# A fused attention, RWKV mix and FFT feed-forward kernel on one core: two variance products placed later, the rows of one pair reordered, and joint visits from group 7 on

## The chip, the core and the metric

The program runs on one core of one Trainium2 chip. The metric is the device time of one launch in microseconds (us). Runs of one program agree within some tenths of a per cent.

## What is computed

The sizes are B = 4 batches, 12 heads, S = 448 tokens, D = 768, and hidden widths of 1024 and 3072. All is float32.

```python
attn = 1 / (1 + exp(-(scale * q @ k.T - log(S))));  x = attn @ v          # per head, heads side by side
xk = mu_k * x + (1 - mu_k) * x_prev;  xr = mu_r * x + (1 - mu_r) * x_prev  # x_prev: one token earlier
x = sigmoid(xr @ w_r) * (relu(xk @ w_k) ** 2 @ w_v)
u = x + real(fft(fft(x, axis=1), axis=2))
un = (u - mean(u)) / sqrt(var(u) + 1e-6)
out = u + relu(un @ w_ch1) @ w_ch2
```

## The kernel before

Tokens lie in the free dimension (448 columns), features in the partitions, in blocks of 128. Nearly every product is done on operands split in two float32r parts, high and low, as three matmuls (high by high, high by low, low by high). A split is one cast on ScalarE (ACT) and one subtraction on VectorE (DVE).

**The order of the work** is written by a planner, the class `Order` (line 136). Pieces of the program are generators. `Order.run` (line 184) wakes those whose time has come on a clock of its own, `now`, and between them issues one matmul of the queue `feed`. A generator yields the time at which it wants to be woken. Each engine executes what was issued to it in exactly that order, whatever the real times are; the real waits are semaphores that come from the data. `need` (line 162) yields until the planner's time of a step, `issued` (line 169) only until the step has been issued. So a number that is yielded moves instructions in the queues of PE, ACT, DVE and SP (which issues the transfers), and nothing else.

**The stages**, in order of time: attention with the key products `k`, the receptance products `r`, the value products `v`, the Fourier part, the normalisation, the first feed-forward product `f`, and the second one `m`. The value products of batches 0 to 3 run from 343 us on, with the Fourier work of the batch before among them.

*The value and Fourier part, per batch b.* `val_done` (line 832) multiplies a finished `v` tile by the receptance tile `rv`, loaded by `load_r` (line 784), which frees the tile's PSUM bank. `folds` (line 880) forms the operands `xf`, `yf` on DVE and their parts `xh`, `xl`, `yh`, `yl`. `spectrum` (line 970) issues the matmuls `pa`, `qa` (on those parts), `pq`, `sp`, then the product `mu` with a matrix of ones, for the mean. `centre` (line 1039) subtracts the mean, squares, and adds the squares up in `sum_v`. `scale` (line 1073) splits `sum_v` into a tile `sq`, issues the two matmuls `var` with the ones, and computes `rs` = 1/sqrt by one ACT function and one Newton step on DVE. Then `centre` multiplies six blocks by `rs` (`x<-x,rs`), one after the other, each waiting for the one before. For batch 1, `load_un` (line 774) splits each of these blocks into `un`, the operand of the next stage. The ones at lines 1079 and 1080 are what the change touches.

*The first feed-forward product.* There are 12 groups of 256 hidden columns (`NG`). Groups 0 to 3 (`PL = 4`) of batches 0 and 1 are done plainly (`plain`, line 1342, tiles named `f`, 18 matmuls each): 16 tiles. All else runs on pairs of batches with Strassen's scheme, seven products of half-size blocks instead of eight: pair 0 is batches 0 and 1, pair 1 is batches 2 and 3. A visit is one group for one pair (63 matmuls) or for both (126 matmuls, a joint visit). The list `VISITS` (line 131) holds visits of pair 0 alone (groups `PL` to `JO`-1), then joint visits (groups `JO` to 11), then visits of pair 1 alone (groups 0 to `JO`-1); before, `JO` is 8. `visit_loads` (line 1276) fetches a group's weights, 2 tiles `a` of 384 KB. `visits` (line 1296) forms sums of their blocks on DVE (`s`, `a`) and splits the seven operands `blk`. It is a generator of its own, so it prepares the first two operands of visit 0 as soon as their weights have landed. `plain_done` and `after` (line 1367) move results from PSUM through ACT and DVE to staging tiles `h`, `w`, `u`, and store them (`h_d`). The staging tiles of pair 1 have one buffer each.

*The rows of a pair* are the other operands. `rows0` (line 1200) prepares pair 0. `rows1` (line 1232) prepares pair 1 from whole half-batches of 1344 columns: B11 and B21 as they are, then T1, T3, T2 and T4 from differences, and B22. Its helper `split` waits for the cast, then for the subtraction, before the next step is issued. T4 and B22 go through DRAM (`t_d`), since their place is needed.

*The second part of the weights.* `convert_rest` (line 1644) rewrites 48 halves of w_ch2 (raw 384 KB each) into operands `v_d` in DRAM. It starts when visit `JO - PL` has its second weight tile, with at least 3.5 us from one half to the next on the planner's clock. When the last product of pair 0 is done (`LAST0`, line 132, the end of visit 7), the loads for the second product (`w`, `r`) and three more places for weights of visits are set free at once.

Of the kernel before, what the change touches and what calls it, by code (L numbers as in the profile page):

```python
# [12 lines left out]
F32 = mybir.dt.float32  # L13
F32R = mybir.dt.float32r
# [3 lines left out]
ALU = mybir.AluOpType  # L18
# [3 lines left out]
B, H, S, DH = 4, 12, 448, 64  # L22
# [4 lines left out]
KD = D // 128  # L27
# [10 lines left out]
NV = 3  # L38
TURNS = (2, 4)
EVERY = (9.0, 10.3)  # L40
PL, JO, EARLY = 4, 8, 8

SL = np.r_[np.arange(2, 129, 2), np.arange(1, 128, 2)]
LL = np.r_[0, np.arange(130, 255, 2), np.arange(129, 256, 2)]
# [236 lines left out]
def build(tc, ap):  # L281
    nc = tc.nc
    V, G = nc.vector, nc.gpsimd
    o = Order(nc)
    est = ExitStack()

    def pool(stack, name, bufs=1, side="left", space=None):
        if space is not None:
            return stack.enter_context(tc.tile_pool(name=name, bufs=bufs, space=space))
        return stack.enter_context(tc.tile_pool(name=name, bufs=bufs, side=side, reuse_waits="tile"))  # L290

    def shift(pl, name, n=1):
        pl.tile([128, int(16 * n)], F32, tag=f"shift_{name}", name=f"shift_{name}", bufs=1)
# [70 lines left out]
    t_d = [dram.tile([128, 3, S], F32, name=f"t_d{i}") for i in range(2)]  # L364
# [259 lines left out]
    for f in range(NF + KD):  # L624
        if f < NF:
            src, hl, key = ap["w_k"][f], [w[:, f].rearrange(flat) for w in (wkh, wkl)], ("wk", f)
        elif f < NF + HELD:
            src, hl, key = ap["w_r"][f - NF], [w.rearrange(flat) for w in wr_t[f - NF]], ("wr", f - NF)
# [46 lines left out]
    def bank2(name):  # L675
        return ps1b.tile([128, 512], F32, tag="bank2", name=name)
# [73 lines left out]
    def split(t, key, raw):  # L750
        yield o.act(t[:, 0], raw)
        o.at[key] = o.sub(V, t[:, 1], raw, t[:, 0])
        yield o.now
# [53 lines left out]
    np_ = pool(s_r, "norm", 1, "right")  # L807
# [67 lines left out]
    def ft(b, tag, shape, dtype=F32, bufs=1, pl=None):  # L875
        return (pl or fp).tile(shape, dtype, tag=tag, name=f"{tag}_{b}", bufs=bufs)
# [162 lines left out]
    def centre(b, ps):  # L1039
# [6 lines left out]
        for i in range(3):  # L1046
# [12 lines left out]
            yield o.act(sq, xx, AF.Square)  # L1059
            add_up(b, "v", i, sq)  # L1060
        yield from scale(b)
        rs = rs_t[b]
        for i in range(KD):
# [9 lines left out]
    def scale(b):  # L1073

        yield from o.need(("v", b, 2))
        hl = ft(b, "sq", [128, 2, S], F32R, pl=np_)
        v = sp_t[b]["v"]
        yield o.act(hl[:, 0], v)
        yield o.sub(V, hl[:, 1], v, hl[:, 0])
        ps = bank2(f"var_{b}")  # L1080
        for c in range(2):
            o.mm(ps[:, 0:S], one, hl[:, c], c == 0, c == 1)
        yield o.now + 0.1
        vs = ft(b, "sq", [128, 2, S], pl=np_)
        vv, sd = vs[:, 0], vs[:, 1]
        rs = rs_t[b] = np_.tile([128, S], F32, tag="rsb", name=f"rs_{b}", bufs=1)
        yield o.ts(vv, ps[:, 0:S], 1.0 / D, 1e-6, ALU.mult, ALU.add)
        o.spend(nc.scalar, 1.3)
        yield o.act(rs, vv, AF.Abs_reciprocal_sqrt)
        yield o.act(sd, rs, AF.Square)  # L1090
        o.tt(V, sd, sd, vv, ALU.mult)
        o.ts(sd, sd, -0.5, 1.5, ALU.mult, ALU.add)
        t = o.tt(V, rs, rs, sd, ALU.mult)
        o.at["scaled", b] = o.now
        yield t
# [5 lines left out]
    blk_t, t_t, plain_t = {}, {}, {}  # L1101
# [48 lines left out]
    def quarter(name, dtype=F32R):  # L1150
        return wq.tile([128, D], dtype, tag="wq", name=name, bufs=4)
# [79 lines left out]

    def rows1():
        def split(nm, hi, lo, src):
            yield o.act(hi, src)
            t = o.sub(V, lo, src, hi)
            for d in range(3):
                t_t[1, nm, d] = (hi[:, d], lo[:, d])
                o.at["t", 1, nm, d] = t
            yield t

        def new(nm):
            t = tp1.tile([128, 2, 3, S], F32R, name=f"{nm}_1")
            return t[:, 0], t[:, 1]

        yield from o.need(("centre", 2))
        u = x2_t[2]
        b11, b21 = u[:, 0:3], u[:, 3:6]
        yield from split("B11", *new("B11"), b11)
        yield from split("B21", *new("B21"), b21)
        yield from o.need(("centre", 3), ("rows", 0))  # L1250
        v = x2_t[3]
        b12, b22 = v[:, 0:3], v[:, 3:6]
        o.dma(t_d[1], b22)
        yield o.tt(V, b11, b12, b11, ALU.subtract)
        t1 = np_.tile([128, 2, 3, S], F32R, tag="x2", name="T1_1", bufs=3)
        yield from split("T1", t1[:, 0], t1[:, 1], b11)
        yield o.tt(V, b12, b22, b12, ALU.subtract)
        yield from split("T3", *new("T3"), b12)
        yield o.tt(V, b12, b22, b11, ALU.subtract)
        yield from split("T2", *new("T2"), b12)  # L1260
        yield o.tt(V, b21, b21, b12, ALU.subtract)
        yield o.dma(t_d[0], b21) + 2.0
        for i, nm in enumerate(("T4", "B22")):
            t = np_.tile([128, 2, 3, S], F32R, tag="x2", name=f"{nm}_1", bufs=3)
            yield o.dma(t[:, 1].bitcast(F32), t_d[i]) + 0.5
            yield from split(nm, t[:, 0], t[:, 1], t[:, 1].bitcast(F32))
        shift(tp1, "tp1")
        o.at["rows", 1] = o.now

    wt_t, place_t = {}, {}  # L1270
    for v, (g, ps) in enumerate(VISITS):
        for j in range(2):
            i = 2 * (v - NG + PL) + j
# [22 lines left out]
    def visits():  # L1296

        n = D // 2
        for v in range(len(VISITS)):
            yield from o.need(("wt", v, 0), ("wt", v, 1))  # L1300
            wa, wb = wt_t[v, 0], wt_t[v, 1]
            a11, a12, a21, a22 = wa[:, 0:n], wa[:, n:D], wb[:, 0:n], wb[:, n:D]
            s3 = al.tile([128, n], F32, tag="sw", name=f"s34_{v}", bufs=1)
            src = {"A11": a11, "S2": a11, "S3": s3, "S1": a21, "A12": a12, "A22": a22, "S4": s3}
            t = {"S3": o.tt(V, s3, a11, a21, ALU.subtract), "S1": o.tt(V, a21, a21, a22, ALU.add)}
            for k, (nm, _, _) in enumerate(PRODUCTS):
                m = 7 * v + k
                yield t.get(nm, o.now)
                if m > 5:
                    yield from o.need(("prod", m - 6))  # L1310
                elif m > 1:
                    yield from o.need("plain loads", ("pl", 2 * PL - 2 + (m > 3), 1, KD - 1))
                if m % 6 < 2:
                    blk = alb.tile([128, D], F32R, tag="blk", name=f"blk_{m}", bufs=2)
                else:
                    blk = quarter(f"blk_{m}")
                blk_t[m] = blk
                yield o.act(blk[:, 0:n], src[nm])
                o.at["blk", m] = o.sub(V, blk[:, n:D], src[nm], blk[:, 0:n])
                if nm == "A11":  # L1320
                    t["S2"] = o.tt(V, a11, a21, a11, ALU.subtract)
                elif nm == "A12":
                    o.at["wt free", v, 0] = t["S4"] = o.tt(V, s3, a12, a11, ALU.subtract)
                elif nm == "A22":
                    o.at["wt free", v, 1] = o.at["blk", m]
        o.at["visits"] = o.now
# [274 lines left out]
    o.spawn(rows0())  # L1601
    o.spawn(visit_loads())
    o.spawn(visits())
    o.spawn(network())
    o.run(("four", B - 1))
    s_f.close()
    s_b = ExitStack()
    tp1 = pool(s_b, "tp1", 1, "right")
# [44 lines left out]

    o.spawn(convert_rest())
    o.spawn(rows1())
    o.run(("prod", LAST0))
    s_t.close()
# [85 lines left out]
```

## Time and profile before

| | us |
|---|---|
| median of three runs (1141.53 to 1143.3) | 1141.82 |
| the profiled execution | 1139.96 |
| its span, first to last instruction | 1138.2 |
| PE busy in the span | 1118.6 (98%) |
| PE weight loads busy | 975.0 (86%) |
| DVE busy | 810.6 (71%) |
| ACT busy | 649.2 (57%) |

Some 1.8 us of the profiled execution lie around its span. The 5908 matmuls are pipelined, each has a busy time longer than its distance to the next, so a stall is read from the starts of neighbouring matmuls, or from the column of the idle time, and not from the busy share. The granted clock is at its upper level (2.4 GHz, written 1.00) but for two stretches, read below at 0.50 (1.2 GHz).

### The profile page before, as it was taken

Reading aid. Unit: us, or ns where it says so; the run is one execution under the profiler, and the core shown is the slowest. Engines: PE = TensorE matmul, PEld = TensorE weight load, DVE = VectorE, ACT = ScalarE, POOL = GpSimd, SP = SyncE. Lnnn points to the kernel's source line nnn. Section 1 sums busy time; section 2 is a strip of 40 time slices with the busy share of each in tenths; the row PEclk is TensorE's granted clock in tenths of the full one; section 3 lists DMA queues with packets and bytes.
Section 4 is the critical chain, followed back from the end, with each engine's and each line's share of the span. In section 5 each row is a group of like instructions: output and inputs, shape, how many; then the busy total and the mean of one; then the engine's idle time right before and its main releaser. Section 6 shows DMA issues by size and latency. Waiting matters only on the chain.

```text
span 1138.2 us, 16784 instructions
## 1 busy us (share of the span) xinstructions
PE 1118.6 (98%) x5908; PEld 975.0 (86%) x5908; DVE 810.6 (71%) x1306; ACT 649.2 (57%) x1165; POOL 16.1 (1%) x49
## 2 busy tenths in 40 slices
PE   9999999999999999989999999989999999999998
PEld 3476676799999989979999999879999999999997
DVE  3876767566624678799896565677657679976887
ACT  6788877766632333334686666667755444554442
POOL 0000001100000000000000000000000000000000
PEclk9999999999999999999999999999999999999999
DMA  7765789667939786536967988999887448945432
GB/s 247 237 231 202 241 325 342 256 231 262 335 136 313 278 305 226 179 134 227 298 230 249 301 300 276 319 318 360 271 332 267 135 151 283 360 145 184 160 99 86
DMA packets 116309, 279.65 MB, mean 246 GB/s; under 512 B 13248, under 2 KB 58496, under 8 KB 116096
## 3 DMA queue, kind: packets, MB, share of 16 engines
q1 hardware_dynamic: 113472, 266.29, 68.4%
q0 software_dynamic: 2464, 11.83, 2.8%
q8 instruction: 46, 0.75, 0.3%
q10 hardware_dynamic: 288, 0.46, 0.1%
q14 instruction: 39, 0.32, 0.1%
HBM read 184.80 MB, written 93.73 MB: 245 GB/s over the span
## 4 chain that ended last, share of the span: by engine, by line
PE 88%; DVE 5%; DMA 4%; ACT 2%; issue 1%; SPq 0%; DVEq 0%; ACTq 0%
PE m L213 23%; PE k L213 9%; PE f_Y L213 9%; PE v L213 8%; PE r L213 8%; PE av L213 6%; PE f_X L213 6%; PE f_W L213 6%; PE sc L213 5%; PE f L213 4%; PE pq L213 1%; PE sc_c L213 1%; DVE out L248 1%; PE pa L213 1%; PE qa L213 1%
## 5 line engine op out<-in xcount | busy, mean ns | idle before, releaser
L213 PE MATMUL m<-hs,sw 128*128 128x448 f32 x1512 | 303.7, 362 | 0.9 <-DVE hs L248 0.8
L213 PEld LDWEIGHTS m<-hs,sw 128*128 128x128 f32 x1512 | 283.3, 188 | 21.1 <-DVE hs L248 2.0
L265 ACT CAST sw<-w 128x768 fp32r<-128x768 f32 x84 | 70.0, 833 | 90.7 <-PE m L213 50.3
L265 ACT CAST hs<-r 128x896 fp32r<-128x896 f32 x84 | 78.9, 940 | 65.3 <-DVE r L248 65.3
L248 DVE TENSOR_TENSOR sw<-w,sw 128x768 fp32r<-128x768 f32 x84 | 80.2, 955 | 49.2 <-ACT sw L265 49.0
L213 PE MATMUL v<-k,wvh 128*128 128x448 f32 x384 | 111.5, 365 | 0.0
L248 DVE TENSOR_TENSOR hs<-r,hs 128x896 fp32r<-128x896 f32 x84 | 91.3, 1087 | 5.9 <-ACT hs L265 5.9
L267 ACT ACTIVATE sg<-sc,bias_s 128x448 f32<-128x448 f32 x144 | 78.3, 649 | 12.5 <-PE sc L213 12.4
L213 PE MATMUL f_Y<-T,blk 128*128 128x448 f32 x360 | 78.8, 367 | 4.3 <-ACT u L265 3.5
L213 PE MATMUL f_W<-T,blk 128*128 128x448 f32 x360 | 77.9, 364 | 0.4 <-DVE blk L248 0.4
L213 PEld LDWEIGHTS f_Y<-T,blk 128*128 128x128 f32 x360 | 68.1, 190 | 10.0 <-ACT u L265 4.2
L213 PEld LDWEIGHTS v<-k,wvh 128*128 128x128 f32 x384 | 71.9, 188 | 4.8 <-issue 0.4
L213 PEld LDWEIGHTS f_W<-T,blk 128*128 128x128 f32 x360 | 67.9, 189 | 5.4 <-DVE blk L248 0.8
L213 PE MATMUL k<-xkh,wkh 128*128 128x448 f32 x192 | 70.7, 368 | 0.9 <-ACT kt L267 0.9
L213 PE MATMUL k<-xkl,wkh 128*128 128x448 f32 x192 | 70.3, 366 | 0.0
L213 PE MATMUL v<-k,wvl 128*128 128x448 f32 x192 | 70.0, 365 | 0.0
L213 PE MATMUL k<-xkh,wkl 128*128 128x448 f32 x192 | 70.0, 364 | 0.0
L213 PE MATMUL f<-un,w1h 128*128 128x448 f32 x192 | 57.1, 374 | 4.5 <-DVE un L248 2.7
L267 ACT ACTIVATE w_raw<-w_raw 128x384 f32<-128x384 f32 x80 | 44.3, 553 | 23.9 <-DMA w_raw<-in_w 23.9
L213 PE MATMUL av<-sg,v 128*64 128x448 f32 x288 | 57.2, 544 | 0.0
L265 ACT CAST blk<-a 128x384 fp32r<-128x384 f32 x80 | 40.4, 513 | 28.3 <-PE f_Y L213 7.8
L256 DVE SCALAR_TENSOR_TENSOR w<-w_raw,w 128x384 uint32<-128x384 uint32 x60 | 33.3, 555 | 28.6 <-ACT w L267 24.6
(200 smaller groups left out, 2071.1 us busy)
## 6 DMA issues: line engine op xcount, KB each, us to landing
w<-v_d SPq DMA_DIRECT2D x84, 384.0 KB, 3.2
w_raw<-in_w SPq DMA_DIRECT2D x80, 384.0 KB, 4.6
r<-h_d SPq DMA_DIRECT2D x48, 448.0 KB, 5.8
k_d<-kp SPq DMA_DIRECT2D x32, 448.0 KB, 3.9
k<-k_d SPq DMA_DIRECT2D x32, 448.0 KB, 6.1
h_d<-h SPq DMA_DIRECT2D x56, 224.0 KB, 4.2
a<-w_d SPq DMA_DIRECT2D x32, 384.0 KB, 5.0
v_d<-w SPq DMA_DIRECT2D x48, 192.0 KB, 4.7
```

The lines of the kernel that those rows point to most:

```text
L213: self.nc.tensor.matmul(out, lhs, rhs, start=start, stop=stop, skip_group_check=skip)
L248: eng.tensor_tensor(out, a, c, op=op)
L256: self.nc.vector.scalar_tensor_tensor(out, a, scalar, c, op0=op0, op1=op1)
L265: self.nc.scalar.copy(out, a)
L267: self.nc.scalar.activation(out, a, fn, **kw)
```

## The change

There are four edits.

- `JO` goes from 8 to 7. Group 7 is then visited jointly, instead of once for each pair. `VISITS` has 15 entries instead of 16: three of pair 0, five joint, seven of pair 1. The matmuls are the same: 20 times 63 in visits.
- In `scale`, the step between the split of `sum_v` and the two `var` matmuls yields a time 3.0 us later for batches 0 and 1.
- `rows1` no longer waits for each part: `split` issues the cast and spawns the subtraction, T3 and T2 come before T1, two differences are issued together, T4 and B22 wait 4.0 us of the planner's clock before their loads, and the start waits for `rows0` to be issued only.
- `visits` first waits for the tile of chunk 6 and batch 0 of the plain groups.

```diff
-PL, JO, EARLY = 4, 8, 8
+PL, JO, EARLY = 4, 7, 8
@@ scale
-        yield o.sub(V, hl[:, 1], v, hl[:, 0])
+        yield o.sub(V, hl[:, 1], v, hl[:, 0]) + 3.0 * (b < 2)
@@ rows1
         def split(nm, hi, lo, src):
-            yield o.act(hi, src)
-            t = o.sub(V, lo, src, hi)
-            for d in range(3):
-                t_t[1, nm, d] = (hi[:, d], lo[:, d])
-                o.at["t", 1, nm, d] = t
-            yield t
+            t = o.act(hi, src)
+
+            def low():
+                t = o.sub(V, lo, src, hi)
+                for d in range(3):
+                    t_t[1, nm, d] = (hi[:, d], lo[:, d])
+                    o.at["t", 1, nm, d] = t
+                yield t
+
+            o.spawn(low(), t)
+            return t
...
+        def late(nm, i):
+            t = np_.tile([128, 2, 3, S], F32R, tag="x2", name=f"{nm}_1", bufs=3)
+            yield o.dma(t[:, 1].bitcast(F32), t_d[i]) + 0.5
+            split(nm, t[:, 0], t[:, 1], t[:, 1].bitcast(F32))
+
...
-        yield from split("B11", *new("B11"), b11)
-        yield from split("B21", *new("B21"), b21)
-        yield from o.need(("centre", 3), ("rows", 0))
+        split("B11", *new("B11"), b11)
+        yield split("B21", *new("B21"), b21)
+        yield from o.need(("centre", 3))
+        yield from o.issued(("rows", 0))
         v = x2_t[3]
         b12, b22 = v[:, 0:3], v[:, 3:6]
         o.dma(t_d[1], b22)
-        yield o.tt(V, b11, b12, b11, ALU.subtract)
+        t = o.tt(V, b11, b12, b11, ALU.subtract)
+        t = o.tt(V, b12, b22, b12, ALU.subtract)
+        yield t
+        split("T3", *new("T3"), b12)
+        yield from o.issued(("t", 1, "T3", 0))
+        t = o.tt(V, b12, b22, b11, ALU.subtract)
+        yield t
+        split("T2", *new("T2"), b12)
+        t = o.tt(V, b21, b21, b12, ALU.subtract)
         t1 = np_.tile([128, 2, 3, S], F32R, tag="x2", name="T1_1", bufs=3)
-        yield from split("T1", t1[:, 0], t1[:, 1], b11)
-        yield o.tt(V, b12, b22, b12, ALU.subtract)
-        yield from split("T3", *new("T3"), b12)
-        yield o.tt(V, b12, b22, b11, ALU.subtract)
-        yield from split("T2", *new("T2"), b12)
-        yield o.tt(V, b21, b21, b12, ALU.subtract)
+        split("T1", t1[:, 0], t1[:, 1], b11)
+        yield t
         yield o.dma(t_d[0], b21) + 2.0
+        shift(tp1, "tp1")
         for i, nm in enumerate(("T4", "B22")):
-            t = np_.tile([128, 2, 3, S], F32R, tag="x2", name=f"{nm}_1", bufs=3)
-            yield o.dma(t[:, 1].bitcast(F32), t_d[i]) + 0.5
-            yield from split(nm, t[:, 0], t[:, 1], t[:, 1].bitcast(F32))
-        shift(tp1, "tp1")
+            yield o.now + 4.0
+            yield from late(nm, i)
         o.at["rows", 1] = o.now
@@ visits
         n = D // 2
+        yield from o.need(("pl", 2 * PL - 2, 0, KD - 1))
         for v in range(len(VISITS)):
```

## Rows read from the trace of the kernel before

**Rows 1.** The page, part 1: busy us, share of the span, instructions, by engine.
```profile
PE 1118.6 (98%) x5908; PEld 975.0 (86%) x5908; DVE 810.6 (71%) x1306; ACT 649.2 (57%) x1165; POOL 16.1 (1%) x49
```

**Rows 2.** Stretches: length, busy us (instructions) of PE, PEld, DVE, ACT, POOL; clock; DMA; GB/s.
```profile
480.00:512.00 32.00, 27.08 (x135) 24.03 (x135) 31.56 (x72) 11.06 (x23) 0.00 (x0) 0.95 0.38 126
545.00:556.00 11.00, 11.00 (x57) 10.31 (x55) 10.86 (x21) 7.93 (x16) 0.00 (x0) 1.00 0.97 323
556.00:570.00 14.00, 14.00 (x72) 13.13 (x71) 10.32 (x17) 7.68 (x15) 0.00 (x0) 1.00 0.89 280
570.00:582.00 12.00, 12.00 (x62) 11.25 (x61) 11.29 (x19) 11.18 (x25) 0.00 (x0) 1.00 0.93 308
582.00:597.00 15.00, 14.50 (x73) 13.25 (x72) 14.72 (x22) 10.88 (x20) 0.00 (x0) 1.00 0.51 175
...
722.00:762.00 40.00, 35.30 (x165) 31.56 (x164) 27.11 (x51) 25.26 (x53) 0.00 (x0) 0.96 0.97 349
```

**Rows 3.** The chain that ended last: start us, us, what; one product of a visit.
```profile
569.36 1.80 PE f_X L213 x9
```

**Rows 4.** Timeline of PE at the variance of batch 0: start, us, what [idle before].
```profile
420.74 0.37 PE L213 MATMUL v<-k,wvl 128*128 128x448 f32 x1
423.28 0.47 PE L213 MATMUL var<-sq,one 128*128 128x448 f32 x1 [2.17 <-ACT sq L265]
424.29 0.47 PE L213 MATMUL var<-sq,one 128*128 128x448 f32 x1 [0.54 <-DVE sq L248]
...
425.41 0.35 PE L213 MATMUL pa<-cd,xh 128*113 128x198 f32 x2
```

**Rows 5.** Timeline of DVE at the same place.
```profile
420.75 0.62 DVE L248 TENSOR_TENSOR x<-v,rv 128x448 f32<-128x448 f32 x1 [4.60 <-DMA rv<-r_d]
...
423.62 0.61 DVE L248 TENSOR_TENSOR sq<-sum_v,sq 128x448 fp32r<-128x448 f32 x1
...
424.69 0.37 DVE L248 TENSOR_TENSOR xl<-xf,xh 128x225 fp32r<-128x225 f32 x1
```

**Rows 6.** Timeline of PE where the plain groups begin.
```profile
496.15 0.68 PE L213 MATMUL f<-un,w1h 128*128 128x448 f32 x2 [1.81 <-DVE x L248]
...
503.92 0.71 PE L213 MATMUL f<-un,w1h 128*128 128x448 f32 x1
507.34 0.47 PE L213 MATMUL f<-un,w1h 128*128 128x448 f32 x1 [2.71 <-DVE un L248]
```

**Rows 7.** Timeline of DVE there: a multiply by rs, a bank's release, visit 0, un.
```profile
491.14 0.62 DVE L248 TENSOR_TENSOR x<-x,rs 128x448 f32<-128x448 f32 x1
491.68 0.62 DVE L248 TENSOR_TENSOR un<-x,un 128x448 fp32r<-128x448 f32 x1
...
495.48 0.62 DVE L248 TENSOR_TENSOR x<-v,rv 128x448 f32<-128x448 f32 x1
...
500.95 0.55 DVE L248 TENSOR_TENSOR s<-a,a 128x384 f32<-128x384 f32 x1
...
503.79 0.56 DVE L248 TENSOR_TENSOR a<-a,a 128x384 f32<-128x384 f32 x1
...
506.67 0.62 DVE L248 TENSOR_TENSOR un<-x,un 128x448 fp32r<-128x448 f32 x1
```

**Rows 8.** Stretches, columns as in rows 2: after the wait at 507 us.
```profile
508.10:511.40 3.30, 3.30 (x10) 2.91 (x9) 3.30 (x9) 2.23 (x5) 0.00 (x0) 0.50 0.00 0
```

**Rows 9.** Timeline of DVE before visit 2: a split of the second pair, an operand.
```profile
593.39 1.55 DVE L248 TENSOR_TENSOR T<-x,T 128x1344 fp32r<-128x1344 f32 x1
594.86 0.55 DVE L248 TENSOR_TENSOR blk<-a,blk 128x384 fp32r<-128x384 f32 x1
```

**Rows 10.** Timeline of PE: the wait for an operand at visit 2.
```profile
595.47 1.68 PE L213 MATMUL f_X<-un,blk 128*128 128x448 f32 x7 [0.50 <-DVE blk L248]
```

**Rows 11.** Timelines of PE and ACT in the first visits of pair 1 alone.
```profile
746.46 3.29 PE L213 MATMUL f_Y<-T,blk 128*128 128x448 f32 x9 [2.98 <-ACT u L265]
...
736.82 0.54 ACT L267 ACTIVATE h<-f_Y 128x448 f32<-128x448 f32 x1 [2.92 <-DMA h_d<-h]
```

## The prediction

> **What bounds the kernel now.** I read the busy shares first, then the stretches, then the timelines at each hole between matmuls. PE carries the time: it is busy for 98% of the span [rows 1], and a product of nine matmuls takes 1.80 us [rows 3], so one matmul has a pitch of 0.20 us. The change leaves all 5908 matmuls in place, so it can only fill holes. The reader should see four groups of them behind the attention stage.
>
> (1) The first `var` matmul of batch 0 starts 2.54 us after the matmul before it, the second 1.01 us after the first [rows 4]. Less the pitch, these are 2.34 and 0.81, together 3.15 us. The reason is one DVE instruction: `x<-v,rv` stood 4.60 us at the head of the DVE queue for its transfer, and the split of `sum_v` came behind it, at 423.62 [rows 5].
>
> (2) Where the plain groups begin, PE waited 1.81 us for a bank that `x<-v,rv` frees, and then, from 504.12 (the start at 503.92 and one pitch) to 507.34, 3.22 us for the third block of `un` of batch 1 [rows 6]. DVE is the bound there: 31.56 of 32 us busy [rows 2]. Behind the second wait the granted clock is 0.50, and 10 matmuls take the 3.30 us that 16 would need at full clock [rows 8]. With its two ends, which the row leaves out, the stretch at that level costs some 1.7 us.
>
> (3) Two short waits for operands of visits, 0.50 us at visit 2 [rows 10] and a smaller one at visit 4. Ahead of the first stands a subtraction of `rows1` of 1.55 us, and the operand right behind it [rows 9].
>
> (4) In the first visits of pair 1 alone PE runs 165 matmuls in 40 us, where 200 would fit: 7.0 us lost [rows 2]. The longest wait there is 2.98 us, for ACT, and ACT stood 2.92 us for a store `h_d<-h`; the matmuls behind the long wait ran slowly, nine in 3.29 us [rows 11].
>
> **The change part by part.**
>
> *`var` of batch 0, 3.0 us later.* Taken alone this takes away 3.15 us: 15 `v` matmuls would go first. But between the `var` pair and `pa` of batch 1 only four `v` matmuls stand in PE's queue (from 424.29 + 0.20 to 425.41 is 0.92 us, four or five pitches [rows 4]). `pa` is issued when its own operands are ready by the planner, whatever `var` does. So in the new order PE does the `v` matmuls that fill the place of the pair and those four, six in all, up to 420.94 + 1.20 = 422.14, and then meets `pa`, whose last operand `xl` comes from 424.69 + 0.37 = 425.06 [rows 5]. The stall is passed on. If `pa` as a whole waits for it, PE starts it at 425.1 instead of 425.41: 0.3 us gained. If its first six matmuls can go on the earlier parts (0.6 us, and a `v` of 0.2 us behind them), 1.1 us. If nothing in it waits, 3.0 us. I take 1.1, the middle case, and keep 0.3 and 3.0 as ends. The trace does not tell which parts `pa` waits for, since in it `pa` always came late enough. What hides the later mean of batch 0: its `un` is not needed before 492 us.
>
> *`var` of batch 1, 3.0 us later.* Its matmuls had no wait. Behind it lies the chain of six `x<-x,rs`, each of which gets in line behind what DVE has been given meanwhile. By the costs in the code, the Newton step then falls behind the first additions of the spectrum, and the first multiply falls behind `evod`. So the first two blocks of `un` come about 5 us later in DVE's order, and the bank's release (495.48, [rows 7]) gains the places of the multiply at 491.14 and of the `un` at 491.68, some 0.54 us each from start to start, 1.1 us. The wait at 496.15 shrinks by that. The third block keeps its place behind the same work. For the whole step: nothing lost or gained at the third block, with an end at 5.3 us lost if the whole chain slides.
>
> *Preparing visit 0 later.* Four DVE instructions of visit 0, from 500.95 to 503.79, lie ahead of the `un` at 506.67 on which PE waits [rows 7]. They take two stretches of 1.06 us between neighbours, 2.1 us. They now come after chunk 6, near 558 us, with half a microsecond of a fifth. There DVE has 14.00 - 10.32 = 3.7 us free [rows 2], and the first visit needs them at 569 us, so I cost them at nothing; without that cover they would cost 2.6 us. So `un` is done some 2.0 to 2.1 us sooner, and PE resumes at about 505.3: **2.0 us**. This contains the 1.1 us at the bank, since the third block sets the end of both. The idle time before it is then about 2.65 us (the bank is free sooner, `mu` is done at 502.7) instead of 3.22. The waits written as 2.71 and 2.98 us [rows 6, 11] were followed by the 0.50 level, those of 2.17 and 1.81 us [rows 4, 6] were not. The 3.22 us from start to start is the wait written as 2.71, so 2.65 us would be written as about 2.15. That is near those without a fall, so I take it that the clock stays up, **1.7 us**; the other end is zero.
>
> Here a page speaks against me. The Trainium skill ("TensorE: Matmul & The Clock Gate", section What's actually happening) says that the gate judges activity in windows that run on without regard to the kernel, so where a gap lies counts beside its length. By it 2.65 us could trip the gate as well, and the sum would be 3.1 instead of 4.8; no row here decides it.
>
> *`rows1` without its chain.* The same nine casts and subtractions and four differences, so no work is saved. Between 570 and 597 us DVE is busy for 26.0 of 27 us [rows 2], and seven instructions of 1.47 us net come from here. Packed more closely, up to two more of them stand ahead of the operand of visit 2: at worst 2.9 us more wait there, at best the 0.50 us goes. Later operands gain what these lose, as the sum of DVE's work up to the end of visit 2 is the same. I take zero.
>
> *Joint from group 7 on.* One visit's preparation goes: 7 casts, 7 subtractions and 4 sums, 768 KB. PE waits for none of it now. T3 to B22 are needed from 12.6 us sooner (seven products of 1.80), but the last two have 18 us of joint visit before their turn. The conversion of w_ch2 starts 12.6 us sooner, and `LAST0` comes 12.6 us later, yet both still overlap, for some 75 us instead of 100. The burst of loads at `LAST0`, behind which stores of one-buffer tiles wait, is the same. So I leave the 7.0 us where they are: zero, from 5 gained (the long wait and its slow stretch go) to 5 lost (once more the same).
>
> **Sum.** 1.1 + 2.0 + 1.7 = 4.8 us off the span of 1138.2. The profiled execution was 1139.96, 1.8 of it outside the span, and the median is 1.9 above that; the gain is the same for both. 1141.8 - 4.8 = 1137.0.
>
> **Rivals.**
>
> *The stall is only passed on.* PE waits just as long for `pa`, and the clock falls behind `un` all the same: 0.3 + 2.0, 1139.5. For it: DVE and not PE sets both places [rows 2, 5]. The Trainium skill ("Perfetto Trace Analysis", section Identifying the Most-Contended Engine) has one work on the busiest engine first; by that rule, moving `var` in PE's order brings nothing, and only the visit's preparation counts. 0.22.
>
> *The transfers fall otherwise at `LAST0`.* A store that is issued a little sooner spares the 2.98 us and its slow stretch: 4.8 + 4.7, 1132.3. Against it: the DMA share there is 0.97 [rows 2]. 0.13.
>
> *The rows crowd out the operands.* Two more subtractions of 1.47 us ahead of visit 2, 2.9 us, and a wait of 3.4 us in all would put the clock down for 1.7: 4.8 - 4.6, 1141.6. For it: DVE is full there. 0.15.
>
> *Slower: the chain of batch 1 slides.* If all six multiplies move by the 5.3 us of the first, `un` comes 5.3 - 2.1 = 3.2 us later and the clock falls anyway: 1141.8 - 1.1 + 3.2 = 1143.9. It decides as soon as `un` is later than 507.3 + 1.1. Against it: the multiplies that follow wait behind work that the first ones no longer lengthen. 0.10. A second long wait at `LAST0` (+4.9, 1141.9) has 0.05.
>
> **How the numbers follow.** The forecast has 0.35. A measurement of this kernel tells 0.2% (2.3 us) from no change, so faster means under 1139.5. Forecast and the `LAST0` gain are faster, the passed stall lies on the edge and gives half: 0.35 + 0.13 + 0.11, with some of the crowding cases that stay small, 0.60. Same: the other half, the crowding, the second wait: 0.28. Slower 0.12. The range reaches from 1132.8, the `LAST0` gain nearly, to 1143.0, which leaves out the worst of the slide.
>
> **What would show it.** `var` of batch 0 without a wait, and `pa` with one of 1 to 3 us in its place; if `pa` has none, the first step was too small. PE resuming on `un` near 504 to 505.5 with the clock at 1.00 behind it. The four instructions of visit 0 near 558 us. No new wait above 1 us between 570 and 605. In the 40 us behind `LAST0`, about 165 matmuls. A PE wait at `un` later than 507 would make the forecast wrong, and so would a changed count behind `LAST0`.

## Result: slower, not faster

| | before | after |
|---|---|---|
| median, runs on the same chip | 1141.67 us (1140.99 to 1143.30, 4 runs) | 1149.24 us (1148.98 to 1150.77, 4 runs) |
| ratio, 95% interval | | 1.0073 (1.0058 to 1.0088) |
| profiled execution, its span | 1139.96, 1138.2 | 1149.29, 1147.5 |
| mean granted clock over the span | 0.997 | 0.991 |

The forecast was 1137.0, the range ended at 1143.0. The change costs 0.73% instead of giving 0.4%. One of the 24 executions of the kernel before that go with four of the runs below took 2862.98 us, and the ratios leave it out.

### The profile page after: what moved, and what is told of

Its sections match the earlier page's. It is cut to its first block, busy times and chain, and to the rows that moved or that the text cites. A ratio compares the mean times of both kernels' runs of the same rounds, so it can differ in the third digit from the quotient of the medians.

```text
span 1147.5 us, 16744 instructions
## 1 busy us (share of the span) xinstructions
PE 1124.1 (98%) x5908; PEld 980.2 (85%) x5908; DVE 805.4 (70%) x1295; ACT 647.1 (56%) x1158; POOL 17.1 (1%) x49
## 4 chain that ended last, share of the span: by engine, by line
PE 87%; DVE 7%; DMA 3%; ACT 2%; issue 1%; SPq 0%; DVEq 0%; ACTq 0%
PE m L213 23%; PE k L213 9%; PE f_Y L213 9%; PE v L213 8%; PE r L213 8%; PE av L213 6%; PE f_W L213 6%; PE f_X L213 6%; PE sc L213 4%; PE f L213 4%; PE pq L213 1%; DMA a<-w_d 1%; PE pa L213 1%; DVE x L248 1%; PE sc_c L213 1%
## 5 line engine op out<-in xcount | busy, mean ns | idle before, releaser
L213 PE MATMUL r<-xrh,wrl 128*128 128x448 f32 x144 | 52.3, 363 | 0.0
```

The costliest lines, as they stand in the source:

```text
L213: self.nc.tensor.matmul(out, lhs, rhs, start=start, stop=stop, skip_group_check=skip)
```

## The profile after

Part 1 of the page of the changed kernel (columns as in [rows 1]):

```profile
PE 1124.1 (98%) x5908; PEld 980.2 (85%) x5908; DVE 805.4 (70%) x1295; ACT 647.1 (56%) x1158; POOL 17.1 (1%) x49
```

The same 5908 matmuls, and a little less work on DVE and ACT than in [rows 1]. So the 9.3 us of span are holes and clock, not work. Where they lie shows when the N-th matmul of both kernels is compared by its start. The changed kernel is 2.7 us ahead behind the place of `var` (near 426 us), level again from 434 to 467 us, 2.2 to 4.1 us late from 471 us on, 4.4 to 4.8 late from 518 us, 9.7 late at 590 us, 8.3 to 8.9 late from 598 to 735 us, and 9.2 late at the end.

The waits of PE between 400 and 800 us in the changed kernel (engine and tile that waited, what it waited for: us in total, times, longest):

```profile
PE f_Y L213 <- ACT u L265: 4.1, 1, 4.1
PE f L213 <- DVE un L248: 3.8, 3, 2.1
PE f_Y L213 <- DVE w L248: 3.5, 2, 2.8
PE v L213 <- DVE x L248: 2.8, 1, 2.8
PE pa L213 <- DVE xl L248: 1.2, 2, 0.8
PE f L213 <- DVE x L248: 1.0, 1, 1.0
```

The wait at `var` [rows 4] is gone as intended, and a smaller one stands at `pa`. New are the wait of `v` for a bank (2.8 us) and that of `f_Y` for `w` (2.8 of the 3.5 us). PE's timeline in the changed kernel has them in these lines (start us, us, engine, line, operation; in brackets the idle time before it and who ended it):

```profile
422.93 0.35 PE L213 MATMUL pa<-cd,xl 128*113 128x198 f32 x1 [0.80 <-DVE xl L248]
424.65 0.39 PE L213 MATMUL pa<-cd,xl 128*113 128x192 f32 x1 [0.45 <-DVE xl L248]
...
470.90 0.68 PE L213 MATMUL v<-k,wvh 128*128 128x448 f32 x2 [2.75 <-DVE x L248]
...
498.42 0.68 PE L213 MATMUL f<-un,w1h 128*128 128x448 f32 x2 [1.04 <-DVE x L248]
...
502.75 0.47 PE L213 MATMUL f<-un,w1h 128*128 128x448 f32 x1 [0.85 <-DVE un L248]
...
509.09 0.47 PE L213 MATMUL f<-un,w1h 128*128 128x448 f32 x1 [2.06 <-DVE un L248]
...
587.75 2.99 PE L213 MATMUL f_Y<-un,blk 128*128 128x448 f32 x9 [2.81 <-DVE w L248]
...
767.66 3.73 PE L213 MATMUL f_Y<-T,blk 128*128 128x448 f32 x9 [4.06 <-ACT u L265]
```

The first two answer [rows 4], the lines from 498.42 to 509.09 answer [rows 6], the last one [rows 11]. The clock behind four of them (window, its length, PE busy, granted clock, DMA share, GB/s):

```profile
424.00:427.00 3.00, 2.55 (x12) 0.64 0.71 213
510.00:517.00 7.00, 6.18 (x28) 0.51 0.00 1
588.00:592.00 4.00, 4.00 (x13) 0.58 0.42 123
766.00:773.00 7.00, 5.34 (x14) 0.51 0.90 284
```

Over the span, a mean of 0.991 is 2 x 0.009 x 1147.5 = 20.7 us at the lower level, against 6.8 us before. Time at half clock loses half of itself where PE has work (as in [rows 8]), so the clock takes up to 6.9 us of the 9.3, and the rest is longer waiting. This is one execution; the experiments below go by the ratios of several.

## Experiments

Each ratio is to the kernel before on the same chip, with its 95% interval, and the us that follow are worked out from the ratio. The differences of the two medians, which some of the expectations use, are up to 1.4 us away from that: 2.8, 3.9, 1.7, -2.3 and -4.6 us for the five edits alone, in the order below. "Alone" means one edit put into the kernel before.

**The edits alone.** The later `var` of batch 0:

```diff
-        yield o.sub(V, hl[:, 1], v, hl[:, 0])
+        yield o.sub(V, hl[:, 1], v, hl[:, 0]) + 3.0 * (b == 0)
```

> The kernel before, with the 3.0 us later var of batch 0 alone. Theory A (the tile of batch 3): the six multiplies by rs of batch 0 each get in line behind more DVE work, so the normalisation of batch 0 ends some 12 us later, the tile x2 of batch 3 is given out only then, and the first two x<-v,rv of batch 3 stand some 8 us later in DVE's order: PE waits 2.5 to 3.5 us for a bank near 468 us, as in the changed kernel. Together with the stall that is passed on to pa and a lower clock behind it: 3 to 5.5 us slower than before, about 1146. Theory B (only the chain of batch 1 matters, the later mean of batch 0 is hidden): no wait above 1 us near 468, time within 1.5 us of before.

Measured 1.0034 (1.0020 to 1.0048), 3.9 us. The new wait is there with this edit alone:

```profile
469.12 1.12 PE L213 MATMUL v<-k,wvh 128*128 128x448 f32 x2 [2.56 <-DVE x L248]
```

Theory A holds. Ahead of this wait the edit did gain: from 430 to 466 us the N-th matmul is 0.9 us further ahead of the kernel before than it was in front of the stall, with the clock at 1.00 in both. The wait and the lower clock behind it then take 5.2 us. The chain can be read on DVE. The multiplies by `rs` of batch 0, first and last, before and then in the changed kernel:

```profile
430.10 0.62 DVE L248 TENSOR_TENSOR x<-x,rs 128x448 f32<-128x448 f32 x1
...
438.87 0.62 DVE L248 TENSOR_TENSOR x<-x,rs 128x448 f32<-128x448 f32 x1
```

```profile
435.95 1.69 DVE L248 TENSOR_TENSOR x<-x,rs 128x448 f32<-128x448 f32 x3
...
450.33 0.62 DVE L248 TENSOR_TENSOR x<-x,rs 128x448 f32<-128x448 f32 x1
```

The delay of 3 us on the planner's clock is 5.9 us at the first multiply and 11.5 us at the last. With the edit alone these begin at 434.36 and 448.75 us, 4.3 and 9.9 us later than before; the changed kernel has the low clock from 424 us on besides. Its last store `c_d<-x` goes out at 454.53 us instead of 439.52, since other transfers stand ahead of it in SP's queue. On that store hangs `("centre", 0)`, and `new_x2` does not give out the tile `x2` of batch 3 before it. `val_done` waits for the tile before it issues `x<-v,rv`. So these land further back in DVE's order. In the kernel before the first two stood at 461.76 and 463.44 us; in the changed kernel:

```profile
469.70 1.15 DVE L248 TENSOR_TENSOR x<-v,rv 128x448 f32<-128x448 f32 x2
```

No line of DVE from 455.61 us to there shows a wait: it works without a pause, and the instruction that frees PE's bank is just late in the queue. That the tile of batch 3 is the link is read from the program and these times; it was not tried by itself.

The later `var` of batch 1 (the same line with `b == 1`):

> The kernel before, with the 3.0 us later var of batch 1 alone. Theory A: no wait near 468 us; the un blocks of batch 1 stand later in DVE's order, so the waits of PE between 496 and 511 us change in place and size; sum between 0 and 2 us slower. Theory B (the chain of batch 1 slides as a whole, up to 5.3 us): un comes 3 to 5 us later and the clock falls as before: 3 to 5 us slower, about 1145 to 1147.

Measured 1.0046 (1.0032 to 1.0061), 5.3 us: Theory B by size, but the wait is not at `un`:

```profile
507.77 1.86 PE L213 MATMUL mu<-sum_u,one 128*128 128x448 f32 x2 [5.58 <-DVE sum_u L248]
```

This one wait stands in the place of three: before, PE waited 1.81 us for the bank and 2.71 for `un` [rows 6], and 0.41 for `mu` at 503.44 us. The two sums are 5.58 and 4.93 us. So most of the loss lies elsewhere in this execution: the granted clock is 0.50 from 506 to 512 us, longer than before [rows 8]; a wait of 1.35 us for `w` is new in visit 1 (at 584.35 us); and some 1.9 us are not of the edit, since the clock fell at 424 us, ahead of where it acts.

Two runs told of further down differ in this delay alone, with the same clock until 507 us: visit 0 later, group 7 joint and the new rows (0.9982), and the same with the later `var` of batch 1 (1.0037). Without the delay `mu` does not wait. With it:

```profile
506.03 1.02 PE L213 MATMUL mu<-sum_u,one 128*128 128x448 f32 x2 [3.45 <-DVE sum_u L248]
```

The addition `sum_u` that it needs begins at 504.70 us instead of 503.39, though PE was 0.8 us ahead up to 495 us and no step of `sum_u`'s own chain was moved. DVE's windows (length, busy, clock, DMA share, GB/s), without and then with the delay:

```profile
470.00:490.00 20.00, 14.74 (x33) 1.00 0.36 127
490.00:510.00 20.00, 19.76 (x45) 1.00 0.46 160
```

```profile
470.00:490.00 20.00, 12.46 (x28) 1.00 0.29 99
490.00:510.00 20.00, 19.76 (x46) 0.93 0.42 147
```

From 490 us on DVE is full in both. In the twenty microseconds before, it did 2.3 us less with the delay. In a stretch where DVE is the bound, work that comes later is not hidden; it is pushed behind 490 us, ahead of or among the operands that PE waits for. The waits of PE from 497 to 511 us are 3.04 us without the delay (1.81 for the bank, 1.23 for `un`) and 3.70 with it (`mu`, and 0.25 for `un`), and a low clock from 507 to 510 us comes with them. In visits 1 and 2 the waits grow from 2.03 to 4.08 us. What carries the lateness on to the visits was not tried.

The new `rows1` (the diff above):

> The kernel before, with the new rows1 alone. Theory A (crowding): the two differences of 1.55 us that are issued together stand ahead of w<-w,f_Y, on which the last product of visit 1 waits; PE waits 2.5 to 3.5 us there, between 582 and 590 us, and 3 us at the lower clock behind it cost another 1.5: 3.5 to 5 us slower, about 1145.5. Theory B (the same work in another order costs nothing, the wait in the changed kernel comes from the 2 us that everything ahead of it is later): no wait above 1 us there, within 1 us of before.

Measured 1.0019 (1.0008 to 1.0029), 2.2 us. In the profiled execution the wait of Theory A is there:

```profile
583.53 3.25 PE L213 MATMUL f_Y<-un,blk 128*128 128x448 f32 x9 [2.76 <-DVE w L248]
```

and DVE shows the pair that is issued together, ahead of `w<-w,f_Y`:

```profile
579.33 1.55 DVE L248 TENSOR_TENSOR x<-x,x 128x1344 f32<-128x1344 f32 x1
580.92 1.56 DVE L248 TENSOR_TENSOR x<-x 128x1344 f32<-128x1344 f32 x1
582.39 0.55 DVE L256 SCALAR_TENSOR_TENSOR w<-w_raw,w 128x384 uint32<-128x384 uint32 x1
582.86 0.61 DVE L248 TENSOR_TENSOR w<-w,f_Y 128x448 f32<-128x448 f32 x1
```

The time lies between the two theories: less than A gave, and more than B allowed. In this execution the wait and the low clock behind it take 4.9 us, and 1.4 of them are back at the end, as two short waits of later visits (0.50 us at visit 2 [rows 10] and 0.24 at visit 4) are gone. That the clock does not fall in each execution may be the rest; it is not shown.

Joint visits from group 7 (`JO = 7`):

> The kernel before, with joint visits from group 7 on alone. Theory A: all stages up to the joint visits stay as they are; the waits at the beginning of the visits of pair 1 alone move by 12.6 us and keep their sum of about 7 us within 1.5 us: within 1.5 us of before. Theory B (the later beginning of the second stage's loads and the earlier conversion leave the burst of transfers with less): 2 us or more, of either sign.

Measured 0.9986 (0.9970 to 1.0003): no difference that can be told from none, leaning to a gain of 1.6 us. That is at the edge of Theory A (1.5 us), and the interval does not exclude Theory B.

Visit 0 prepared later (the one line in `visits`):

> The kernel before, with visit 0 prepared later alone. Theory A (as predicted): four DVE instructions less ahead of the third block of un of batch 1, PE resumes on it some 2 us sooner (at 505.0 to 505.5 instead of 507.34), and the clock stays up or not: 2.0 to 3.7 us faster, 1138 to 1139.8. Theory B (the gain is taken by the next waits, of mu, un and the banks, or by the conversions that DVE does later): within 1 us of before.

Measured 0.9971 (0.9956 to 0.9985), 3.3 us faster. Theory A: `un` of the third block comes 2.0 us sooner (504.65 us against 506.67 [rows 7]), in the profiled execution no wait is left between 496.25 and 508 us, and the N-th matmul is 3.7 us earlier from 509 us on. The wait for the bank, DVE's subtraction, and the clock from 496 to 501 us:

```profile
496.25 0.67 PE L213 MATMUL f<-un,w1h 128*128 128x448 f32 x2 [1.81 <-DVE x L248]
...
504.65 0.62 DVE L248 TENSOR_TENSOR un<-x,un 128x448 fp32r<-128x448 f32 x1
...
496.00:501.00 5.00, 4.75 (x16) 0.66 0.28 111
```

The clock is 1.00 from 501 us on. It fell behind the wait for the bank instead, and slowed PE at a place where it would have had to wait for `un` anyway.

**One edit taken out of the changed kernel.** Without the later `var` of batch 0 (`b == 1` in place of `b < 2`):

> The changed kernel without the later var of batch 0 (that of batch 1 stays). Theory A (the loss near 468 us belongs to batch 0 alone): no wait near 468 us, the stall of 3 us near 421 us is back, net 3 to 5 us faster than the changed kernel, 1144.5 to 1146.5. Theory B (the two delays cost together and not each by itself): within 1.5 us of 1149.2.

1.0037 (1.0019 to 1.0055), 36 ten-thousandths or 4.1 us below the changed kernel's 1.0073. Theory A: no wait near 468 us. Without that of batch 1 (`b == 0`):

> The changed kernel without the later var of batch 1 (that of batch 0 stays). Theory A (what it costs alone, 3.9 us, it costs here too, by un blocks of batch 1 that come later in DVE's order): the waits of PE between 497 and 511 us shrink from 6.3 us in all to 4 or less, 1145 to 1147. Theory B (with visit 0 out of the way DVE has the 2 us there, and the delay costs little): 1147.5 to 1149.5.

1.0013 (0.9998 to 1.0028), 6.9 us below, more than alone. Between 497 and 511 us three gaps of 1.26, 1.21 and 1.88 us from start to start are left, against 1.41, 1.22, 2.42 and 1.21; the low clock from 510 to 517 us and that in visit 1 are gone too. The waits there shrink a little less than Theory A gave (4.4 us are left), and the time by more. With `rows1` as before:

> The changed kernel with rows1 as it was before. Theory A (the rows packed closely cost what they cost alone, 1.7 us, or more behind the later visits 0 to 2): no wait above 1.5 us between 580 and 592 us, 1145 to 1147.5. Theory B (visit 1 is late because of all that is later ahead of it, whatever the rows do): a wait of 2 us or more stays between 580 and 605 us, 1148.5 or more.

1.0046 (1.0031 to 1.0062), 3.1 us below. The wait in visit 1 falls to 1.28 us. Theory A. It falls as far with the new rows kept and the delay of batch 1 taken out: in the run before this one it is 0.72 us, with 1.31 us at a later product. So the 2.81 us of the changed kernel need both.

**Cures of one mechanism.** The multiplies of batch 0 issued together, in the changed kernel:

```diff
             t = o.tt(V, u[:, i], u[:, i], rs, ALU.mult)
-            yield t
+            if b:
+                yield t
```

> The changed kernel, but the six multiplies by rs of batch 0 are issued together, none waiting on the planner's clock for the one before; the 3.0 us are kept. Theory A (the 3.0 us cost because the chain of multiplies stretches them, so that the tile of batch 3 is given out late): c_d is stored by 440 us, x<-v,rv of batch 3 regains its place near 462 us, the wait near 468 us is gone or below 1 us, and the time falls by 3 to 5 us, to 1144 to 1146. Theory B (DVE is just full between 455 and 471 us, whoever is first): a wait of 2 us or more stays there, and the time stays within 1.5 us of the changed kernel's 1149.2.

1.0025 (1.0011 to 1.0038), 5.5 us below the changed kernel. The delay is still in it, but the chain can't stretch:

```profile
436.45 3.29 DVE L248 TENSOR_TENSOR x<-x,rs 128x448 f32<-128x448 f32 x6
```

The three stores follow from 437.63 us, `x<-v,rv` stands at 462.15 and 465.49 us, and no gap above 0.6 us is left between 425 and 497 us. This shows the cause: not the 3.0 us, but what the chain behind them makes of it. The 5.5 us are more than the wait that went; in the two profiled executions the difference is 2.8 us.

The two first differences of `rows1` apart:

```diff
-        t = o.tt(V, b11, b12, b11, ALU.subtract)
-        t = o.tt(V, b12, b22, b12, ALU.subtract)
-        yield t
+        yield o.tt(V, b11, b12, b11, ALU.subtract)
+        yield o.now + 4.0
+        yield o.tt(V, b12, b22, b12, ALU.subtract)
```

> The changed kernel, but the two first differences of rows1 are issued 4 us of the planner's clock apart instead of together. Theory A (the pair of 1.55 us differences ahead of w<-w,f_Y makes the wait of 3.17 us in visit 1 and the low clock behind it): the wait falls under 1.6 us, the clock stays up, the time falls by 2 to 4.5 us, to 1145 to 1147. Theory B (DVE's work up to the end of visit 2 is the same, so the wait only moves to a later operand): the waits between 580 and 605 us keep their sum of some 3 us, within 1.5 us of 1149.2.

1.0078 (1.0058 to 1.0098): nothing gained. The wait in visit 1 falls to 1.29 us, and others take its place:

```profile
583.05 2.08 PE L213 MATMUL f_Y<-un,blk 128*128 128x448 f32 x9 [1.29 <-DVE w L248]
596.45 2.08 PE L213 MATMUL f_Y<-un,blk 128*128 128x448 f32 x9 [0.52 <-DVE w L248]
601.85 1.67 PE L213 MATMUL f_W<-T,blk 128*128 128x448 f32 x7 [1.13 <-DVE blk L248]
610.97 1.28 PE L213 MATMUL f_Y<-un,blk 128*128 128x448 f32 x5 [0.25 <-DVE w L248]
```

3.19 us in all: Theory B. (This execution, 1146.18 us, is the fastest of six; their median is 1150.00.) That the two differences stand side by side is not what costs. That it is the amount of the rows' work in this stretch is likely, and not shown.

**Combinations.** The two gains, and nothing else:

> The kernel before with the two edits that measured as gains when alone: visit 0 prepared later (0.9971) and joint visits from group 7 (0.9986); no later var, rows1 as before. Theory A (they act at different places, near 505 us and behind the last product of pair 0, and add up): 0.9957 of before, 1135.5 to 1138. Theory B (what is gained ahead of the burst of transfers is waited for there again): 1139 to 1141.

0.9965 (0.9951 to 0.9979), 1136.18 us median: faster than both kernels. The 0.9957 of Theory A lies inside the interval. With the new `rows1` added to it:

> Visit 0 later and group 7 joint, with the new rows1 and no later var. Theory A (the rows cost at two places, some 2 us of waits in visits 1 and 2 and, by another order of the transfers, one wait above 4 us with a low clock behind the last product of pair 0): 2 to 4 us above 0.9965 of before, that is about 0.999. Theory B (the rows cost only behind the delays, since these bring DVE's work of two stages together): within 1 us of 0.9965.

0.9982 (0.9969 to 0.9994), about 1.9 us more; the expected 2 us just missed, and the two intervals overlap, but the waits of Theory A are there. With the two differences apart as well:

> The changed kernel without the later var of either batch, and with the two first differences of rows1 issued 4 us of the planner's clock apart instead of together. Theory A (the var delays and the pair of differences are all that costs): no wait near 468 us, none above 1.5 us in visit 1, PE resumes on the third un 2 us sooner, and the joint group's gain of 2.3 us is kept: 4 to 7 us faster than before, 1135 to 1138. Theory B (a part of the loss sits elsewhere in the rows or where the visits of pair 1 begin): 1140 or more.

0.9993 (0.9981 to 1.0005): Theory B; apart or together, the rows cost the gain. In the profiled executions the N-th matmul falls behind by 1.4 us in visits 1 and 2 when the new rows are added to the two gains, and by another 1.8 us behind the last product of pair 0. ACT and PE there, with the old rows (first) and with the new ones, not apart:

```profile
751.98 0.53 ACT L265 COPY w<-f_W 128x448 f32<-128x448 f32 x1 [2.49 <-DMA h_d<-w]
754.43 0.53 ACT L265 COPY u<-f_Y 128x448 f32<-128x448 f32 x1 [1.10 <-DMA h_d<-u]
755.02 2.08 PE L213 MATMUL f_Y<-T,blk 128*128 128x448 f32 x9 [1.71 <-ACT u L265]
```

```profile
755.14 0.53 ACT L265 COPY w<-f_W 128x448 f32<-128x448 f32 x1 [4.44 <-DMA h_d<-w]
757.68 0.53 ACT L265 COPY u<-f_Y 128x448 f32<-128x448 f32 x1 [0.31 <-DMA h_d<-u]
758.26 2.62 PE L213 MATMUL f_Y<-T,blk 128*128 128x448 f32 x9 [3.69 <-ACT u L265]
```

It is the same in all of them: the five runs that join group 7 with the old rows have two or three waits of at most 2.93 us there from start to start and no low clock behind them; the seven with the new rows, the changed kernel among them, have one of 3.85 to 4.80 us and a low clock. What in the rows moves the stores was not tried.

Last, the two gains with the multiplies of batch 0 issued together, without and with the later `var` of batch 0:

> Visit 0 later and group 7 joint, with the six multiplies of batch 0 issued together and no delay. Theory A (the multiplies of batch 0 have room where they are; issued together they hold back what stands behind them by at most 3 us where PE has a store of work): within 1.5 us of 0.9965 of before. Theory B (six multiplies in a row, some 3.3 us, delay an operand that PE waits for): 2 us or more above that, with a new wait between 422 and 440 us.

> Visit 0 later and group 7 joint, with the 3.0 us later var of batch 0 and the six multiplies of batch 0 issued together. Theory A (the stall is passed on to pa and the delay gains at most the second var's 0.8 us): the wait of 2 to 2.5 us stands at pa instead of var, no wait near 468 us, and the time is within 1.5 us of the kernel without the delay (e14). Theory B (as predicted, 1.1 us or more): 1.1 to 3 us below e14.

Without: 0.9948 (0.9936 to 0.9960), 1135.64 us. With: 0.9945 (0.9931 to 0.9959), 1135.37 us. These two are the fastest of all. Without the delay it is 1.9 us below 0.9965, a little more than Theory A allowed, and to the good; but the intervals overlap, and in the profiled executions the N-th matmul of the two is level within 0.5 us from 507 to 750 us, so no gain is shown. The delay itself is worth 0.3 us, which can't be told from nothing: Theory A by size. The intervals do not exclude the 1.1 us of Theory B. In the one with the delay the stall stands at `pa`, with 1.91 us in all:

```profile
423.59 0.35 PE L213 MATMUL pa<-cd,xl 128*113 128x198 f32 x1 [1.46 <-DVE xl L248]
425.32 0.35 PE L213 MATMUL pa<-cd,xl 128*113 128x192 f32 x1 [0.45 <-DVE xl L248]
```

## Why the prediction was wrong

**`var` of batch 0: 1.1 us gained was forecast, 3.9 us lost (alone), 4.1 us (taken out).** That the stall is passed on to `pa` was right, also that `pa` begins with its earlier parts: it waits in two pieces. What it gained at its own place may well have been the 1.1: 0.9 us in the one pair of executions without a low clock there, 0.3 us, with a wide interval, where nothing was lost behind it (0.9945 against 0.9948). The step that failed is the cover: "What hides the later mean of batch 0: its `un` is not needed before 492 us." That names one reader of the normalisation and leaves out the other, the tile of batch 3, which `new_x2` ties to `("centre", 0)`. And the sum priced 3.0 us, where a chain of six steps made 9.9 us of it alone and 11.5 us in the changed kernel. I had written of that stretching for batch 1, and did not apply it to batch 0, where it cost.

The Trainium skill ("Perfetto Trace Analysis", section Identifying the Most-Contended Engine) has one work on the most occupied engine first. The runs agree where DVE is that engine, 31.56 of 32 us busy [rows 2]: taking four instructions out of its way there is worth 3.3 us (0.9971). The place of `var` of batch 0 says nothing on it, though the rival drew on it there: DVE itself stood idle for 4.60 us [rows 5].

**`var` of batch 1: nothing was forecast, with an end at 5.3 us lost; it lost 5.3 us alone, 6.9 us in the changed kernel.** The value taken was wrong, and that the bound of 5.3 held alone is luck, since it was the price of a late `un`. The step looked for the places that the bank's release gains in DVE's order, and took "the third block keeps its place behind the same work". The bank's wait did go, as it said. The step left out `mu`, which waits for DVE too (3.45 to 5.58 us), and the visits behind. And it left out that DVE, 31.56 of 32 us busy [rows 2], can't make up for work that is not done ahead of the full stretch; with the delay that is 2.3 us. The rival of the sliding chain had the right sign and a price of 3.2 us, at a chance of 0.10. Its mark, a wait at `un` later than 507 us, is there in the changed kernel (at 509.09).

**Visit 0 later: 3.7 us forecast, 3.3 us measured.** The 2.0 us of `un` stood. The 1.7 us of the clock came by luck: it was to stay up behind a wait of 2.65 us at the third block, and in the profiled execution it fell earlier, behind the bank, where that cost nothing, and no wait was left at the third block. In the changed kernel the gain does not show, since the waits at `un` there, 3.8 us in all, come in part with the delay of batch 1: without that, 2.4 us are left and the low clock is gone.

**The clock.** I took 1.7 us because a wait of some 2.15 us "is near those without a fall". This rule doesn't hold. In the changed kernel the clock was low behind waits of 0.80 and 0.45 us (0.64 in the window from 424 us). In the kernel without the delay of batch 1 it stayed up behind one of 3.27 us:

```profile
472.15 0.67 PE L213 MATMUL v<-k,wvh 128*128 128x448 f32 x2 [3.27 <-DVE x L248]
...
470.00:475.00 5.00, 2.85 (x14) 1.00 0.62 220
475.00:480.00 5.00, 5.00 (x45) 1.00 0.14 49
```

**`rows1`: zero was forecast, 2.2 us lost alone, 3.1 us taken out.** The argument "later operands gain what these lose" is right for DVE and wrong for PE: a wait is lost when it happens, and the later gain is no use where little was waited for (0.50 and 0.24 us). The rival "the rows crowd out the operands" named the crowding, at 0.15, and a wait of nearly the right size (2.76 us measured, 2.9 forecast). It had the place wrong: two differences of 1.55 us stand ahead of `w` at the end of visit 1, not two subtractions of 1.47 us ahead of an operand of visit 2. Its 4.6 us are what the one execution lost there (4.9), and twice the 2.2 us of the ratio.

**Group 7: zero, with 5 us to either side; 1.6 us gained, not told from zero.** Right within its ends. But the 7.0 us did not all stay where they were. With group 7 joint and the old rows, no low clock follows the last product of pair 0 in five profiled executions; with the first joint visit at group 8 one does in four of five, that of the kernel before among them.

**The sum.** The five edits alone add up to 34 + 46 + 19 - 14 - 29 = 56 ten-thousandths, 6.4 us, against 8.3 us (6.6 to 10.0) for all. So most of it is no odd meeting of edits but two prices of zero and one gain that were losses: 3.9 + 5.3 + 2.2 = 11.4 us against a forecast of -1.1 for the three. Some meeting is not excluded. By differences of medians the five add up to 1.5 us against 7.6 for all, and taken out one by one the three give 4.1 + 6.9 + 3.1 = 14.1 us. In part that is because the wait in visit 1 is counted twice: it goes with the rows and with the delay of batch 1.

## To carry over

When a step is moved in a hand-written order, list all that waits for its last descendant, tiles and buffers of later stages too, and price the chain by its length, not by the shift. Ask first which engine is full where the moved work lands: later work on a full engine is lost time even if its own readers can wait. And judge an edit that bundles several by each one alone: two of these five gave 4 us together, and the other three, each alone, took some 11.

## What was not expected of the hardware

The same stall with the same matmuls behind it is followed by a low clock in one kernel's execution and not in another's. Up to 426 us the kernels of these two runs issue the same instructions in the same order to PE, DVE, ACT and SP. `var` of batch 0 waited 2.31 us in the run with group 7 alone and 2.20 us in the run of 0.9948 (the lines of `var`, then the clock behind them, in that order):

```profile
423.49 0.47 PE L213 MATMUL var<-sq,one 128*128 128x448 f32 x1 [2.31 <-ACT sq L265]
...
424.00:427.00 3.00, 2.50 (x18) 1.00 0.81 301
```

```profile
422.64 0.47 PE L213 MATMUL var<-sq,one 128*128 128x448 f32 x1 [2.20 <-ACT sq L265]
...
424.00:427.00 3.00, 3.00 (x12) 0.50 0.49 177
```

In the run of the two gains, the same there too, the wait was 1.99 us and the clock 0.50 behind it. So of a wait of 2 to 3 us the time lost is only known to within the lower clock behind it, and executions of one kernel differ by that: those of the kernel before went from 1136.36 to 1146.26 us on one chip, with a mean clock of 0.998 and 0.993, which by the sum above is 5.7 of the 9.9 us. By the Trainium skill ("TensorE: Matmul & The Clock Gate", section What's actually happening) activity is judged in windows that run on without regard to the kernel, so that one kernel shows different counts of slow matmuls at its start from run to run. These traces agree, in mid-kernel, with 1.00 and 0.50 behind 2.31 and 2.20 us. So what the prediction drew from that page against its 1.7 us, that a shorter wait can be followed by the lower clock as well, is borne out.
